# Chunk 2 of a fused layernorm + MLP + long convolution enters the MLP already transposed, with row statistics from ScalarE

## The chip, the cores and the metric

One core of one Trainium2 chip. The metric is the time of one execution in microseconds (us); the number given for a kernel is the median over its runs.

## What is computed

All numbers are float32. S = 2048 rows, D = 448 columns, F = 1792 hidden columns.

```python
x  = A_q
xn = layernorm(x)                       # per row: (x - mean) / sqrt(var + 1e-5)
# part A: gated long convolution
k_shift = sum_t pad(k)[t:t+S] * shift_k[:, 3-t]        # causal, 4 taps, per column
kv = k_shift * v
y  = causal_conv(kv, ssm_k) + kv * ssm_D               # length S, per column, by FFT
A  = xn * y
# part B: MLP
h  = xn @ w1 + b1
B  = mish(h) @ w2                       # mish(h) = h * tanh(softplus(h))
out = x + A + B
```

## The kernel before, in words

**The MLP sets the frame.** The 2048 rows are eight chunks of 256 rows, and the 14 blocks of 128 hidden columns are seven pairs, so there are 56 (chunk, pair) steps, each of two *slots*: slot 2i issues step i's first layer (`g1_mm`, line 544, 22 matmuls), slot 2i+1 its activation (`mish`, line 547) and the second layer of step i-2 (`g2_mm`, lines 576 to 578, 12 matmuls). Each product is made from high and low float32r parts, so every operand is split: a copy to the high part on ScalarE, a subtraction for the low part on VectorE (`split`, lines 89 and 90). Chunk c begins at slot 14c; chunk 2 at slot 28.

**The convolution is woven in between.** In slots 6 to 59, eight groups of k and v and eight groups of the filter go through a first transform: `f1_mm` (line 154) multiplies a group into two two-bank accumulators named pq and pr; `f1_fold` then empties them, ScalarE copying one (line 160) and VectorE adding and subtracting the other (line 164, two instructions); `f1_out` stores the result. There is one pair pq, pr for all groups, so the next `f1_mm` waits for the fold before it. VectorE also makes kv from k and v (`taps`, lines 192 to 211); GpSimd multiplies one tap of each group (line 190). In the stretch that matters here the order of the multiplies is: filter group 5 (slot 20), kv group 0 (24), filter group 6 (26), kv group 1 (29). The second stage and the inverse follow from slot 59 on.

**How a chunk gets its normalised, transposed input.** The first layer needs xn with columns on partitions. There are two ways, and `NT` says where the second begins.

- Chunks below NT (0, 1 and 2 before): the chunk is loaded with rows on partitions (`ln_load`). `ln_stats` (line 451) puts the row statistics on VectorE (line 430 twice, 433 twice, 436) into a queue that is emptied between other VectorE instructions; the last entry of the queue gives GpSimd a power, two normalisations and two small copies (lines 439, 443, 447). `ln_T` (line 510) has TensorE transpose the tile in two halves of four instructions each (`transposes`, line 496), and ScalarE and VectorE split it from the accumulator (lines 508, 506).
- Chunks from NT on (3 to 7 before): the rows are still loaded, as the residual and for the statistics, but the transposed chunk comes from a second copy of the input, `qT` (`xT_load`, line 458, into the single tile XN). `nt_stats` (line 460) has ScalarE make two passes over each of the two row blocks, a sum and a sum of squared differences (lines 466 to 468, four large and some small instructions); GpSimd makes the reciprocal root (469, 470) and stores mean and root of all 256 rows, 2 KB, to DRAM (474). `nt_row` (477) loads the 128 pairs of one half back, broadcast to all partitions, into the one tile `idr`. `nt_norm` (483) subtracts and multiplies on VectorE, and `nt_split` (490, 491) makes the two parts. There is a second row load for the second half; it fills the same tile, so it waits until the first half's `nt_norm` has read it.

**What sets the order.** The order on every engine is written out by hand: `at(slot, ...)` calls are issued at the start of a slot and `after(slot, ...)` calls at its end, each engine takes its instructions in that order, and SyncE's queue of loads and stores is one such order. Where the k, v and filter groups are loaded is in lines 628 to 652. The steps of a chunk c from NT on are placed here, from the tables of the diff:

```python
    for c in range(NT, NCHUNK):
        at_ = NT_HOW.get(c, NT_AT)
        b = 2 * NP * (c - 1) + (1 if c < 5 else 0)
        at(b + at_["q"], ln_load, c)
        at(b + at_["x"], xT_load, c)
        after(NT_STATS[c], nt_stats, c)
        for jj in range(2):
            at(b + at_["row"][jj], nt_row, c, jj)
            after(b + at_["norm"][jj], nt_norm, c, jj)
            after(b + at_["split"][jj], nt_split, c, jj)
```

Of the kernel before, what the change touches and what calls it, by code (L numbers as in the profile page):

```python
# [29 lines left out]
I2_AT = {100: ((6, 7, 0, 1), 92, (95, 97, 98, 99), (0, 2, 0, 1)),  # L30
         108: ((2, 3, 4, 5), 101, (104, 105, 106, 107), (0, 1, 0, 1))}
LATE = 2
NT = 3
NT_AT = {"q": -5, "x": -1, "stats": -2, "flush": 0, "row": (4, 8), "norm": (7, 10), "split": (8, 11)}
NT_SOON = dict(NT_AT, row=(4, 5), norm=(4, 7), split=(6, 8))
NT_HOW = {c: dict(NT_SOON) for c in (4, 7)}
NT_HOW[6] = dict(NT_AT, row=(4, 10), norm=(8, 11), split=(9, 13))
NT_HOW[7]["x"] = 0
NT_HOW[3] = dict(NT_SOON, q=-9, stats=-3, flush=-2)
NT_HOW[5] = dict(NT_AT, q=-8, stats=-4, flush=-2)  # L40
NT_STATS = {3: 27, 4: 41, 5: 53, 6: 70, 7: 82}
EVAC_SOON = 2,
WARM_N = (448, 448, 448)
FILL_N = (224, 112, 96)
# [3 lines left out]
def tile_kernel(ctx: ExitStack, tc, q, qT, k, v, sk, hT, sD, w10, w1, w2, c_fib, c_g, c_gi, c_i2, out):  # L48
# [20 lines left out]
    E = dp.tile([NJ * 4, 64, D], F32, name="E")  # L69
    MR = {c: dp.tile([2, CH], F32, name="MR") for c in range(NT, NCHUNK)}  # L70

# [8 lines left out]
    def rs(c):  # L80
        return rstd[:, 2 * c:2 * c + 2] if c < NT else mv[:, 2 * c:2 * c + 2, 1]

# [37 lines left out]
    def at(slot, fn, *args):  # L120
        plan.setdefault(int(slot), []).append((fn, args))

    def after(slot, fn, *args):
        plan2.setdefault(int(slot), []).append((fn, args))
# [294 lines left out]
    def xn_tile():  # L419
        return mp.tile([128, 4, CH], F32, name="xn", bufs=1)  # L420

    def ln_parts(c):
        st = mp.tile([128, 2, 6], F32, name="bst", bufs=2)
        ve = mp.tile([128, 2], F32, name="ve", bufs=2)
        if c < NT:
            XN[c] = xn = xn_tile().rearrange("p a b -> p (a b)").rearrange("p (j d) -> p j d", j=2)
# [83 lines left out]
    def ln_T(c, jj):  # L510
        if jj == 0:
            dv(len(drip))
            x_tiles(c)
        p = pg()
        transposes(c, jj, p)
        for lo in range(2):
            x_split(c, jj, p, lo)
# [73 lines left out]
    def mlp_slot(s):  # L591
# [3 lines left out]
        if half == 0:  # L595
            if i < n:
                c, p = pairs[i]
                if c + 1 < NT:
                    if p == 0:
# [8 lines left out]
        else:  # L608
            if i < n:
                c, p = pairs[i]  # L610
                if p == NP - 2 and c + 1 < NT:
                    ln_T(c + 1, 0)
# [83 lines left out]
# [8 lines that stand above are left out]
# [152 lines left out]
```

## Time and profile before

| What | Value |
|---|---|
| median of 3 runs (lowest to highest) | 357.65 us (357.64 to 357.86) |
| the profiled execution | 357.91 us, span of its instructions 356.1 us |
| VectorE (DVE) busy | 282.0 us, 79% |
| ScalarE (ACT) busy | 160.1 us, 45% |
| GpSimd (POOL) busy | 72.4 us, 20% |
| DMA | 83.27 MB, mean 234 GB/s |
| granted TensorE clock, mean | 1.000 |

How to read it: PE is TensorE, DVE VectorE, ACT ScalarE, POOL GpSimd; SPq, ACTq and POOLq are the queues in which SyncE, ScalarE and GpSimd issue transfers. A row of the timeline has the start in us from the span's first instruction, the duration in us, engine, source line, operation, output<-inputs with their shapes, a count, and in brackets how long the engine was idle before it and what ended the idle time. Neighbouring instructions of an engine overlap a little at their ends, so that the distance from one start to the next is what an instruction costs its engine.

### The profile page before, as it was taken

The page shows a single profiled execution, that of the slowest core. Times are in us where ns is not written, and L with a number is a line of the kernel's source. Part 1 is how long each engine was busy: PE and PEld are TensorE (multiplying, and loading weights), DVE is VectorE, ACT ScalarE, POOL GpSimd, SP SyncE. Part 2 cuts the span into 40 slices and gives each one's busy share as a digit, 9 for nine tenths or more (in the row PEclk, how much of TensorE's full clock was granted, in tenths as well). Part 3 has the DMA queues.
Part 4 walks back from the last instruction along what each step waited for, and adds up shares of the span by engine and source line. Part 5 has one row for each costly group of instructions (what it writes and reads, how often), then busy time and mean ns, then how long its engine had stood idle before and what let it go on. Part 6 is the DMA issues. An engine that isn't in the chain of part 4 may idle for free.

```text
span 356.1 us, 7495 instructions
## 1 busy us (share of the span) xinstructions
PE 350.7 (98%) x3092; PEld 289.1 (81%) x3092; DVE 282.0 (79%) x374; ACT 160.1 (45%) x308; POOL 72.4 (20%) x83
## 2 busy tenths in 40 slices
PE   8999999999999999999999999999999999999995
PEld 2988888888888989888987568657756799979794
DVE  5989748998999999997539868868985963788941
ACT  3975652347343643373232732333634333354470
POOL 2037002822310250222000120110310016040030
PEclk9999999999999999999999999999999999999999
DMA  7999976949769356664859488879756467989086
GB/s 247 344 374 305 401 307 164 352 113 249 209 178 314 127 153 175 218 162 107 246 180 356 135 309 285 254 229 380 257 151 240 105 175 263 407 335 272 17 119 139
DMA packets 30691, 83.27 MB, mean 234 GB/s; under 512 B 3137, under 2 KB 15810, under 8 KB 30658
## 3 DMA queue, kind: packets, MB, share of 16 engines
q1 hardware_dynamic: 21842, 47.82, 39.6%
q0 software_dynamic: 4928, 22.95, 20.3%
q10 hardware_dynamic: 3888, 12.03, 13.1%
q8 instruction: 24, 0.39, 0.4%
q14 instruction: 9, 0.07, 0.1%
HBM read 54.34 MB, written 28.45 MB: 232 GB/s over the span
## 4 chain that ended last, share of the span: by engine, by line
PE 96%; DMA 2%; ACT 1%; SPq 0%; issue 0%; DVE 0%
PE pg L544 23%; PE pg L576 13%; PE pg L578 13%; PE pg L577 13%; PE pa L544 6%; PE pq L544 5%; PE pq L154 4%; PE pa L298 3%; PE pr L544 3%; PE pq L243 3%; PE pr L243 3%; PE pp L544 2%; DMA kr<-in_w_dram 2%; PE pa L243 1%; PE pp L352 1%; PE pb L544 1%
## 5 line engine op out<-in xcount | busy, mean ns | idle before, releaser
L576 PE MATMUL pg<-w2h,ach 128*128 128x448 f32 x224 | 82.2, 367 | 0.0
L578 PE MATMUL pg<-w2h,acl 128*128 128x448 f32 x224 | 81.3, 363 | 0.0
L577 PE MATMUL pg<-w2l,ach 128*128 128x448 f32 x224 | 81.2, 362 | 0.0
L90 DVE TENSOR_TENSOR acl<-a,ach 128x512 fp32r<-128x512 f32 x56 | 38.9, 694 | 34.3 <-ACT ach L89 34.2
L544 PE MATMUL pg<-XH,w1h 128*128 128x256 f32 x264 | 52.9, 284 | 0.1
L552 ACT ACTIVATE a<-pg,b1t 128x256 f32<-128x256 f32 x66 | 27.9, 472 | 55.0 <-PE pg L544 42.9
L576 PEld LDWEIGHTS pg<-w2h,ach 128*128 128x128 f32 x224 | 42.0, 187 | 9.5 <-issue 5.0
L544 PEld LDWEIGHTS pg<-XH,w1h 128*128 128x128 f32 x264 | 41.5, 188 | 7.2 <-issue 5.6
L578 PEld LDWEIGHTS pg<-w2h,acl 128*128 128x128 f32 x224 | 42.0, 188 | 2.5
L577 PEld LDWEIGHTS pg<-w2l,ach 128*128 128x128 f32 x224 | 42.1, 188 | 2.3
L544 PE MATMUL pg<-XL,w1h 128*128 128x256 f32 x264 | 42.9, 277 | 0.0
L164 DVE TENSOR_TENSOR st<-pq,st 128x896 f32<-128x896 f32 x32 | 34.8, 1089 | 4.7 <-ACT st L160 3.9
L544 PEld LDWEIGHTS pg<-XL,w1h 128*128 128x128 f32 x264 | 35.9, 188 | 0.0
L89 ACT CAST ach<-a 128x512 fp32r<-128x512 f32 x56 | 34.8, 621 | 1.7
L544 PE MATMUL pg<-XH,w1l 128*128 128x256 f32 x198 | 33.6, 278 | 0.0
L190 POOL TENSOR_TENSOR x<-kr,skb 128x896 f32<-128x896 f32 x8 | 17.0, 2130 | 71.0 <-PE pr L154 26.2
L309 POOL DMA_DIRECT2D E<-qe x14 | 8.8, 632 | 94.2 <-ACT qe L252 94.2
L207 DVE TENSOR_TENSOR x<-x 128x896 f32<-128x896 f32 x24 | 26.2, 1091 | 2.0 <-POOL x L190 1.4
L544 PEld LDWEIGHTS pg<-XH,w1l 128*128 128x128 f32 x198 | 27.6, 188 | 0.0
L160 ACT COPY st<-pr 128x896 f32<-128x896 f32 x16 | 14.5, 907 | 13.5 <-PE pr L154 11.5
L552 ACT ACTIVATE a<-pa,b1t 128x256 f32<-128x256 f32 x16 | 6.7, 472 | 30.3 <-PE pa L544 30.3
L154 PE MATMUL pq<-x,con 32*64 32x448 f32 x128 | 15.9, 560 | 0.0
(171 smaller groups left out, 639.2 us busy)
## 6 DMA issues: line engine op xcount, KB each, us to landing
Dkv<-st ACTq DMA_DIRECT2D x16, 448.0 KB, 5.2
ah<-Dh SPq DMA_DIRECT2D x8, 896.0 KB, 8.3
av<-Dkv SPq DMA_DIRECT2D x8, 896.0 KB, 8.7
e<-E POOLq DMA_DIRECT2D x8, 896.0 KB, 7.4
E<-qe POOLq DMA_DIRECT2D x14, 448.0 KB, 6.9
kr<-in_k_dram SPq DMA_DIRECT2D x10, 448.0 KB, 6.1
Dh<-st ACTq DMA_DIRECT2D x10, 448.0 KB, 6.8
x<-in_hT_dram SPq DMA_DIRECT2D x8, 448.0 KB, 6.4
```

Of the source, the lines that this page charges most:

```text
L89: nc.scalar.copy(h, raw)
L90: V.tensor_sub(l, raw, h)
L154: nc.tensor.matmul(ps[h][64 * jj:64 * jj + 64, b, :D], f1[rg:rg + 32], x[rg:rg + 32, jj], start=True, stop=True, tile_position=(rg, 64 * jj))
L164: f(st[:, n], e, st[:, 1])
L190: nc.gpsimd.tensor_mul(o, KR[g - u // 2], skb[:, u:u + 1].to_broadcast([128, 2, D]))
L207: V.tensor_add(KV[g], KV[g], o)
L243: nc.tensor.matmul(bk(p, r)[32 * t:32 * t + 32, :D], g[rs, t, c], a[rs, t], start=True, stop=True, tile_position=(64 * r, 32 * t))
L544: nc.tensor.matmul(ps[n], l, r, start=all(m[0] != n for m in seq[:n_]), stop=all(m[0] != n for m in seq[n_ + 1:]))
L552: nc.scalar.activation(a[:, n], ps[n], AF.Mish, bias=b1t[:, 2 * p + n:2 * p + n + 1])
L576: nc.tensor.matmul(ps, ah[:, n, cs], w2h[:, f], start=f == 0, stop=False)
L577: nc.tensor.matmul(ps, ah[:, n, cs], w2l[:, f], start=False, stop=False)
L578: nc.tensor.matmul(ps, al[:, n, cs], w2h[:, f], start=False, stop=f == NF - 1)
```

## The change

`NT` falls from 3 to 2: chunk 2 takes the second way. Its own placing is added. With b = 15 for chunk 2, the rows are loaded at slot 14 (as before), the transposed chunk at slot 16, the statistics are issued after slot 15, the broadcast rows at slots 18 and 21, the normalisations after slots 20 and 22, the splits after slots 22 and 24.

```diff
-NT = 3
+NT = 2
 NT_AT = {"q": -5, "x": -1, "stats": -2, "flush": 0, "row": (4, 8), "norm": (7, 10), "split": (8, 11)}
 NT_SOON = dict(NT_AT, row=(4, 5), norm=(4, 7), split=(6, 8))
 NT_HOW = {c: dict(NT_SOON) for c in (4, 7)}
+NT_HOW[2] = dict(NT_AT, q=-1, x=1, row=(3, 6), norm=(5, 7), split=(7, 9))
 NT_HOW[6] = dict(NT_AT, row=(4, 10), norm=(8, 11), split=(9, 13))
...
-NT_STATS = {3: 27, 4: 41, 5: 53, 6: 70, 7: 82}
+NT_STATS = {2: 15, 3: 27, 4: 41, 5: 53, 6: 70, 7: 82}
```

What goes with it: chunk 2's eight transposes, its statistics on VectorE and its normalisation on GpSimd. What comes: a 512 KB load of `qT`, the two passes on ScalarE, the 2 KB store, two broadcast loads of 128 KB on SyncE's queue, and four VectorE instructions (line 483).

## The prediction

> **What bounds the kernel.** I read the span and clock first, then on the page the engines and the chain that ended last.
>
> ```profile
> core 0: 356.1 us, clock 1.000
> ```
>
> ```profile
> PE 350.7 (98%) x3092; PEld 289.1 (81%) x3092; DVE 282.0 (79%) x374; ACT 160.1 (45%) x308; POOL 72.4 (20%) x83
> PE 96%; DMA 2%; ACT 1%; SPq 0%; issue 0%; DVE 0%
> ```
>
> TensorE is busy 98% of the span and 96% of the chain: from the first steps to the end it waits for nothing. So an edit pays what it takes off TensorE, and costs every pause that it puts there. The profiled execution took 357.91 us, 0.26 above the median of 357.65; I reckon differences in its trace and add them to the median.
>
> **What is removed from TensorE.** TensorE's timeline around the two halves of chunk 2's transposes:
>
> ```profile
> 73.86 0.60 PE L496 MATMUL pg<-con,xn 128*128 128x128 f32 x4
> 74.22 0.45 PE L576 MATMUL pg<-w2h,ach 128*128 128x448 f32 x1
> ...
> 76.81 0.59 PE L154 MATMUL pq<-x,con 32*64 32x448 f32 x2
> ...
> 77.74 0.66 PE L496 MATMUL pg<-con,xn 128*128 128x128 f32 x4
> 78.16 0.60 PE L544 MATMUL pg<-XH,w1h 128*128 128x256 f32 x3
> ```
>
> Start to start, the first half costs 74.22 - 73.86 = 0.36 us and the second 78.16 - 77.74 = 0.42. The saving is 0.8 us, 0.22% of the time; 0.2% (0.72 us) is about what a measurement of this kernel can tell from no change. It stands only if nothing new makes TensorE wait. The row between the halves, 76.81, is the multiply of filter group 6. It writes pq and pr, so it needs the fold of kv group 0 to be over, and this is VectorE's deadline. Without the first half of the transposes TensorE would be there at 76.81 - 0.36 = 76.45.
>
> **How late VectorE can be.** Its timeline from the fold of filter group 5 on:
>
> ```profile
> 57.92 0.62 DVE L430 BATCH_NORM_STATS2 bst<-qt 128x6 f32<-128x448 f32 x1
> ...
> 61.38 1.09 DVE L164 TENSOR_TENSOR st<-pq,st 128x896 f32<-128x896 f32 x1 [1.09 <-ACT st L160]
> ...
> 62.51 1.09 DVE L164 TENSOR_TENSOR st<-pq,st 128x896 f32<-128x896 f32 x1
> 63.51 1.11 DVE L207 TENSOR_TENSOR x<-x 128x896 f32<-128x896 f32 x1
> 64.61 1.05 DVE L90 TENSOR_TENSOR acl<-a,ach 128x512 fp32r<-128x512 f32 x1
> 65.59 0.61 DVE L200 TENSOR_TENSOR x<-kr,skb 128x448 f32<-128x448 f32 x1
> 66.12 0.61 DVE L202 TENSOR_TENSOR x<-kr,skb 128x448 f32<-128x448 f32 x1
> 66.77 1.09 DVE L207 TENSOR_TENSOR x<-x 128x896 f32<-128x896 f32 x1
> 67.89 1.50 DVE L210 TENSOR_TENSOR x<-x 128x896 f32<-128x896 f32 x1
> 69.31 1.08 DVE L197 TENSOR_TENSOR x<-kr,skb 128x896 f32<-128x896 f32 x1
> ...
> 74.27 1.09 DVE L164 TENSOR_TENSOR st<-pq,st 128x896 f32<-128x896 f32 x1
> ```
>
> The last row is the second half of the fold of kv group 0; it ends at 75.36. From 61.38 on no idle time stands in these rows: VectorE works without a break towards a deadline that, at 76.45, is 1.1 us away. The row at 69.31 is the first instruction of kv group 1 and the first to read that group's k.
>
> **What the change adds there.** The same steps of chunk 3 show the price:
>
> ```profile
> 103.82 1.41 DVE L483 TENSOR_TENSOR xn<-xn,con 128x512 f32<-128x512 f32 x2
> 105.16 1.08 DVE L164 TENSOR_TENSOR st<-pq,st 128x896 f32<-128x896 f32 x1
> ...
> 112.44 0.68 DVE L491 TENSOR_TENSOR XL<-xn,XH 128x512 fp32r<-128x512 f32 x1
> 113.04 1.41 DVE L483 TENSOR_TENSOR xn<-xn,con 128x512 f32<-128x512 f32 x2
> ```
>
> One half's normalisation takes 105.16 - 103.82 = 1.34 us of VectorE and one low part 113.04 - 112.44 = 0.60. By the slots, the first normalisation (after 20) goes in behind the add at 63.51; the first low part and the second normalisation (both after 22) behind the instruction at 69.31. So 1.34 + 0.60 + 1.34 = 3.28 us come in ahead of the deadline. The low parts replace two that were made from the accumulator later and are no new work, but the first is now earlier than the deadline. Some time is given back, because GpSimd no longer normalises beside VectorE:
>
> ```profile
> 63.51 2.77 POOL L443 TENSOR_SCALAR xn<-qt,mv,rstd 128x448 f32<-128x448 f32 x1
> ```
>
> Beside it the subtraction at 64.61 took 65.59 - 64.61 = 0.98, where 0.60 is usual for its shape (112.44), and the multiply at 67.89 took 1.42, where 62.51 to 63.51 shows 1.00. That is 0.8 us. The statistics that leave VectorE (57.92 and its like) lie ahead of the wait at 61.38, which ScalarE's copy ends, so that they buy nothing later.
>
> **ScalarE's two passes** come in front of the copy that empties filter group 4:
>
> ```profile
> 47.46 0.94 ACT L89 CAST w2h<-x 128x896 fp32r<-128x896 f32 x1
> 49.47 0.91 ACT L160 COPY st<-pr 128x896 f32<-128x896 f32 x1 [1.07 <-PE pr L154]
> ...
> 83.29 0.58 ACT L466 ACTIVATE a<-qt 128x448 f32<-128x448 f32 x1 [0.75 <-DVE st L164]
> ...
> 86.53 0.19 ACT L468 ACTIVATION_READ_ACCUMULATOR a<-qt,mv 128x1 f32 x1
> ```
>
> For chunk 3 they take from 83.29 to 86.72, 3.4 us. Issued behind the cast of 47.46 they run from 48.4 to 51.8, and the copy of 49.47 and VectorE's fold behind it are 2.3 us late. VectorE meanwhile has two statistics less (2 x 0.6) and the 1.09 us of waiting at 61.38: together 2.3, so this delay is covered at about nothing; without that cover it would add up to 1 us to what follows.
>
> **The row's way and who stands behind it.** First SyncE's queue; then GpSimd's store of chunk 3, and five answers on the time from issue to landing, in this order: of the stores, of the row loads up to 141 us, of the one k load issued at 105.64, of all k loads, and of the loads of qT.
>
> ```profile
> 56.43 0.35 SPq L589 DMA_DIRECT2D out_dram<-qt  x1
> 60.66 0.33 SPq L414 DMA_DIRECT2D qt<-in_q_dram  x1
> 61.51 0.42 SPq L180 DMA_DIRECT2D kr<-in_k_dram  x1
> ...
> 94.72 0.33 SPq L477 DMA_DIRECT2D con<-MR  x1
> ...
> 105.26 0.32 SPq L477 DMA_DIRECT2D con<-MR  x1
> 105.64 0.83 SPq L180 DMA_DIRECT2D kr<-in_k_dram  x1
> ```
>
> ```profile
> 88.81 0.85 POOL L474 DMA_DIRECT2D MR<-mv  x1 [0.30 <-POOL mv L470]
> DMA to landing us min/median/max: 3.7/6.0/7.3
> DMA to landing us min/median/max: 3.0/4.8/5.5
> DMA to landing us min/median/max: 5.6/5.6/5.6
> DMA to landing us min/median/max: 3.5/6.1/13.2
> DMA to landing us min/median/max: 4.1/9.4/10.0
> ```
>
> For chunk 3 the store follows the end of the passes by 88.81 - 86.72 = 2.1 us; here it goes out at 53.9, lands at 59.9 (57.6 to 61.2), and only then can SyncE issue the first row, which lands 4.8 later, at 64.7 (60.6 to 66.7). VectorE is ready for it at 64.5. So the first normalisation runs from 64.7 to 66.0. All that while SyncE's queue stands still, with slot 18's row at its head. Chunk 0's output (56.43) goes out at 60.1, and the load of chunk 3's rows (60.66), which needs that tile, about 64.3. Then comes the second row load (slot 21): it fills the tile that the normalisation reads, so it waits until 66.0, exactly as 105.26 waits for the end of 103.82's pair. Behind it in the queue stands the k load of kv group 1 (slot 22): 61.51 before, 66.4 now. With the 5.6 us of the load that went out behind a row at 105.64 it lands at 72.0; with the bounds 3.5 and 6.1 (the median of all) at 69.9 to 72.5. I take 5.6, being the same position in the queue.
>
> VectorE gets to kv group 1 at 66.0 + (69.31 - 64.61) - 0.8 = 69.9. It waits 2.1 us, until 72.0 instead of 69.31: 2.7 late. With the low part and the second normalisation the fold is 2.7 + 0.60 + 1.34 = 4.6 late and ends at 80.0. TensorE, ready at 76.45, pauses 3.5 us.
>
> **The sum.** Multiply of filter group 6 at 80.0 instead of 76.81: +3.2 (the first half of the transposes is swallowed in it). Second half: -0.4. Total +2.8: 360.7 for an execution like the profiled one, 360.4 on the median. What follows is late by the same amount and not by more: in this order VectorE waits at the end of kv group 1 for ScalarE again, so that its lag ends there. The load of qT (slot 16) stands in the queue ahead of the row's wait; issued at any time before 54 it is there at 64.7 even with the longest landing of its kind, 10.0 us, and costs nothing; issued later it would join the row's lateness.
>
> A rule of the Trainium skill bears on a pause of that length. "TensorE: Matmul & The Clock Gate", section "The HAM clock gate (the 'warmup' mystery)", says that after an idle window of about 3.4 us the clock falls to half until TensorE has been busy for as long. By that rule the sum would be about 1.7 us more, +4.5. The granted clock here is 1.000 in the mean, and no row of before shows a pause of this kind, so the rule is untried in this case; my sum goes without it.
>
> **The rivals.**
>
> - *The k load is in time* (lands by 69.9). Then only VectorE's added work counts: 3.28 - 0.8 = 2.5 late, or 2.7 with the row at 64.7, the fold ends at 77.8 to 78.0, and the total is +0.6 to +0.8 with the saving, or +0.5 with an earlier row: 358.2 to 358.4, about no change to slightly slower. For it: the fastest k load took 3.5 us. Against: chunk 3's rows of q, a filter group and this k now start within 2 us of each other. 0.21, of it 0.13 within 0.2%.
> - *The fold is in time* (ends by 76.45), and the whole 0.8 us stays: 356.8, faster. VectorE would need 1.4 us beyond the 1.1 of slack and the 0.8 given back, and the k load in time as well. It could come from GpSimd's leaving: all of VectorE's instructions from 62 to 71 us ran beside it, and I have credited two. It decides at 76.45. 0.17, of it 0.15 faster.
> - *Store and row are slow* (7.3 and 5.5): the first normalisation ends at 68.0, the k load at 6.1 lands at 74.5, the total is +5.3: 363.0. 0.07.
> - *The clock drops* for about as long as the pause, 3.5 us at half pace: another 1.8 us, 362.2. For it: a pause of this length is nowhere in the trace, so that nothing shows the clock holding through one. Against: it is 1.000 in the mean. The length at which it decides isn't to be had from these rows. 0.05. (The page of the Trainium skill named above puts it at about 3.4 us.)
>
> **How the numbers follow.** My forecast has 0.50, its own range 359.0 to 361.2. Faster is the second rival's 0.15; within 0.2% is 0.13 + 0.02; slower is 0.08 + 0.50 + 0.07 + 0.05 = 0.70. The range from 356.7 to 361.8 holds the forecast and the first two rivals and leaves out the last two, with the forecast's tail.
>
> **What would show it.** Right: no transpose (line 496) for chunk 2; a pause of TensorE of about 3.5 us ahead of line 154 near 76 us, released by VectorE's line 164; ahead of that VectorE idle for about 2 us at line 197, released by the k load; SyncE issuing the row of line 477 near 60 and near 66, the k load directly behind the second. Wrong: line 154 starts near 76.4 with no pause (the second rival), or the pause is there without the wait on the k load (the first), or VectorE waits for the row itself at line 483 by more than a microsecond (the third).

## The result, and the profile after

The changed kernel takes 364.36 us (median of 5 runs, 362.72 to 365.03) against 357.65: slower by 1.8%, ratio 1.0176, interval 1.0164 to 1.0189. The profiled execution took 364.8 us. Executions of this kernel, and of several below, differ among themselves by whether the granted TensorE clock falls after a pause; each such number therefore stands with the clock of its execution. Of these five, 362.72 and 363.35 us ran at a mean clock of 0.995 and 364.36 to 365.03 at 0.991.

Span and clock first; then from the page the engines, the chain that ended last and the granted clock in 40 slices.

```profile
core 0: 362.7 us, clock 0.991
```

```profile
PE 352.6 (97%) x3084; PEld 290.0 (80%) x3084; DVE 282.5 (78%) x373; ACT 163.2 (45%) x318; POOL 65.7 (18%) x81
...
PEclk9999999987999999999999999999999999999999
...
PE 91%; DMA 3%; DVE 3%; issue 1%; SPq 0%; ACT 0%
```

TensorE has eight instructions fewer, the transposes, and yet is busy 1.9 us longer; a DMA and VectorE have come into the chain; and the clock dips in two slices, between 72 and 91 us. TensorE's timeline at the multiply of filter group 6 (at 76.81 before), and VectorE's from the fold of filter group 5 to the end of that of kv group 0:

```profile
81.20 1.01 PE L155 MATMUL pq<-x,con 32*64 32x448 f32 x2 [4.71 <-DVE st L165]
```

```profile
61.46 2.22 DVE L165 TENSOR_TENSOR st<-pq,st 128x896 f32<-128x896 f32 x2 [1.41 <-ACT st L161]
63.59 1.08 DVE L208 TENSOR_TENSOR x<-x 128x896 f32<-128x896 f32 x1
64.59 1.41 DVE L484 TENSOR_TENSOR xn<-xn,con 128x512 f32<-128x512 f32 x2
...
68.83 1.09 DVE L211 TENSOR_TENSOR x<-x 128x896 f32<-128x896 f32 x1
73.19 1.09 DVE L198 TENSOR_TENSOR x<-kr,skb 128x896 f32<-128x896 f32 x1 [3.27 <-DMA kr<-in_k_dram]
74.20 0.68 DVE L492 TENSOR_TENSOR XL<-xn,XH 128x512 fp32r<-128x512 f32 x1
74.81 1.41 DVE L484 TENSOR_TENSOR xn<-xn,con 128x512 f32<-128x512 f32 x2
...
80.06 1.09 DVE L165 TENSOR_TENSOR st<-pq,st 128x896 f32<-128x896 f32 x1
```

VectorE enters kv group 1 late (line 198, 69.31 before) because k isn't there: 3.27 us without work. The normalisation of 74.81 and the low part of 74.20 follow, so the fold ends at 81.15 instead of 75.36 and TensorE pauses 4.71 us. Where k was: SyncE's queue, and behind it GpSimd's store and ScalarE's passes.

```profile
56.74 0.33 SPq L478 DMA_DIRECT2D con<-MR  x1
57.28 0.41 SPq L590 DMA_DIRECT2D out_dram<-qt  x1
63.41 0.33 SPq L415 DMA_DIRECT2D qt<-in_q_dram  x1
...
66.03 0.33 SPq L478 DMA_DIRECT2D con<-MR  x1
66.41 0.43 SPq L181 DMA_DIRECT2D kr<-in_k_dram  x1
```

```profile
52.94 0.81 POOL L475 DMA_DIRECT2D MR<-mv  x1 [0.29 <-POOL mv L471]
```

```profile
48.13 0.57 ACT L467 ACTIVATE a<-qt 128x448 f32<-128x448 f32 x1
...
51.46 0.88 ACT L161 COPY st<-pr 128x896 f32<-128x896 f32 x1
```

The second row load waits for the normalisation that begins at 64.59, and the k load goes out right behind it at 66.41, 4.9 us later than before. Last, the stretch from 76 us on (columns: window, its length, busy time of PE, PEld, DVE, ACT and POOL, PEclk, DMA share, GB/s):

```profile
76.00:78.00 2.00, 0.49 (x3) 0.12 (x1) 1.97 (x5) 1.72 (x4) 0.00 (x0) 1.00 0.32 129
78.00:80.00 2.00, 0.00 (x0) 0.00 (x0) 2.00 (x3) 0.26 (x1) 0.85 (x1) 0.95 0.00 0
80.00:82.00 2.00, 0.80 (x8) 0.33 (x16) 1.85 (x3) 0.00 (x0) 1.23 (x1) 0.50 0.00 0
82.00:84.00 2.00, 2.00 (x21) 1.07 (x6) 2.00 (x4) 0.89 (x1) 0.00 (x0) 0.50 0.33 38
84.00:86.00 2.00, 2.00 (x11) 2.00 (x11) 1.93 (x4) 0.01 (x1) 0.00 (x0) 0.50 0.94 372
86.00:88.00 2.00, 2.00 (x14) 1.96 (x13) 1.97 (x3) 0.54 (x2) 0.00 (x0) 0.85 0.85 309
```

The eighth column is the clock: half from 79.8 (a tenth of the second window) to 86.6, 6.8 us in all, although TensorE works again from 81.2.

**Where the 6.9 us lie.** Comparing the starts of the same matmuls in the two traces: 0.17 early up to 56 us, 0.07 late from 57, 0.38 early at 75 (the first transposes saved), 4.39 late at the multiply of filter group 6, 6.42 late behind the half clock, and 6.41 to 6.49 from there to the end. So all of the loss but the 0.24 us at 57 arises between 76 and 88 us. The pause makes 4.39; the half clock makes 6.42 - 4.39 + 0.42 (the second transposes, saved there too) = 2.45. The span is 6.6 longer, and the remaining 0.3 lies outside it.

### The profile page after: what moved, and what is told of

It reads as the page before. It is cut to its first block, busy times and chain, and to the rows that moved or that the text cites. A ratio compares the mean times of both kernels' runs of the same rounds, so it can differ in the third digit from the quotient of the medians.

```text
span 362.7 us, 7491 instructions
## 1 busy us (share of the span) xinstructions
PE 352.6 (97%) x3084; PEld 290.0 (80%) x3084; DVE 282.5 (78%) x373; ACT 163.2 (45%) x318; POOL 65.7 (18%) x81
## 4 chain that ended last, share of the span: by engine, by line
PE 91%; DMA 3%; DVE 3%; issue 1%; SPq 0%; ACT 0%
PE pg L545 22%; PE pg L577 12%; PE pg L579 12%; PE pg L578 12%; PE pa L545 6%; PE pq L545 5%; PE pq L155 4%; PE pa L299 3%; PE pr L545 3%; PE pr L244 3%; PE pq L244 3%; PE pp L545 2%; DMA kr<-in_k_dram 2%; DMA x<-in_hT_dram 2%; PE pa L244 1%; DVE st L165 1%
## 5 line engine op out<-in xcount | busy, mean ns | idle before, releaser
L578 PE MATMUL pg<-w2l,ach 128*128 128x448 f32 x224 | 81.2, 362 | 0.0
L155 PE MATMUL pq<-x,con 32*64 32x448 f32 x128 | 16.7, 586 | 4.8 <-DVE st L165 4.7
```

The lines of the kernel that those rows point to most:

```text
L155: nc.tensor.matmul(ps[h][64 * jj:64 * jj + 64, b, :D], f1[rg:rg + 32], x[rg:rg + 32, jj], start=True, stop=True, tile_position=(rg, 64 * jj))
L578: nc.tensor.matmul(ps, ah[:, n, cs], w2l[:, f], start=False, stop=False)
```

## Experiments

The theory after this comparison: the time is lost in two steps. The fold of kv group 0 is late, because VectorE has 3.3 us more to do ahead of it with 1.1 to spare, and because the k load is held in SyncE's queue; and the pause then halves the clock. The rivals: that one of the two causes does it alone, that ScalarE's passes delay the chain from the start, and that the clock had nothing to do with it. Each experiment names the times of before that shared its chip. Three of the sixteen expectations met the time that they gave (filler4, hold_alone, row2_behind_k); the other thirteen kernels came out slower than expected. A trace is of one execution, and already at 20 us its matmuls start up to 0.6 us earlier or later than those of before.

### The clock by itself

**filler4**: the changed kernel with four idle products in the pause.

```diff
     def f1_mm(src, g, key):
         x = src.pop(g)
+        if (key, g) == ("h", 6):
+            warmer = pg()
+            for _ in range(4):
+                nc.tensor.matmul(warmer[0:8, 0:448], wz, wz[:, 0:1].to_broadcast([128, 448]), start=True, stop=True)
```

> The changed kernel with four idle multiplies (448 columns of zeros, about 0.75 us each, result unused) ahead of the multiply of filter group 6, in the pause. Theory (the pause halves the clock for some microseconds after it, and this costs about 2.4 us beside the pause itself): the pause ends where it did, the granted clock stays 1.0, time 361.5 to 362.3. Rival (the lower clock costs nothing by itself, the pause and VectorE's lag are the whole loss): time within 0.5 us of 364.4.

Measured: 361.68 us (361.05 to 362.08), before 357.74, ratio 1.0105 (1.009 to 1.012). TensorE stands idle for only 0.4 us and keeps its clock, 0.998 or more in all four executions. The profile is of the fastest; TensorE's wait and VectorE's timeline:

```profile
PE pq L159 <- DVE st L169: 0.4, 1, 0.4
```

```profile
72.05 1.09 DVE L202 TENSOR_TENSOR x<-kr,skb 128x896 f32<-128x896 f32 x1 [2.07 <-DMA kr<-in_k_dram]
...
78.92 1.09 DVE L169 TENSOR_TENSOR st<-pq,st 128x896 f32<-128x896 f32 x1
```

By the medians the half clock cost 364.36 - 361.68 = 2.7 us and the late fold the other 3.9. In this execution k landed sooner than in the profiled one of the changed kernel: VectorE waits 2.07 us for it instead of 3.27, and the fold ends at 80.01 instead of 81.15. The two profiled executions differ by 364.8 - 361.05 = 3.75 us; less these 1.14, the half clock is 2.6, near the 2.45 of the trace. This execution, with k in use 5.6 us after its issue and the clock full, is also the prediction's own sum put to the test: the fold was forecast to end at 80.0.

### One part of the change on the kernel before

**vector_alone**: VectorE's added work and nothing else; the products are not used.

```diff
+    def extra(n):
...
+        o, i = XS[2][1][:, :, 0:128], skb[:, :, 0:128]
+        m = skb[:, 1, 0:256].rearrange("p (a t) -> p t a", t=2)[:, 0:1].to_broadcast([128, 4, 128])
+        for _ in range(n):
+            V.tensor_tensor(o, i, m, op=ALU.mult)
...
+    after(20, extra, 2)
+    after(22, extra, 3)
```

> The kernel before with five VectorE multiplies of 128x512 added, two after slot 20 and three after slot 22 (at some 0.65 us each about 3.2 us, the added VectorE work of the change), written into a tile that chunk 2 doesn't use yet; the results are unused and everything else, the transposes too, stays as before. My theory: VectorE's deadline at the multiply of filter group 6 had about 1.1 us to spare, so this work alone makes a pause of about 2 us at that multiply, 359.4 to 359.9, with the k load on time (issued near 61.5) and, the pause being under 2.5 us, the full clock; one half-clock window would make it 360.6 to 361.2. Rival, that VectorE's work is hidden and only the late k load costs: no pause at line 154, under 358.2.

Measured: 360.1 us (359.78 to 361.97), before 357.77, ratio 1.0077 (1.0051 to 1.0103). Three executions at a clock of 0.999 or more took 359.8 to 360.2; the profiled one, at 0.995, took 361.97. TensorE's pause, a short wait behind it and the windows of that one:

```profile
78.92 0.59 PE L154 MATMUL pq<-x,con 32*64 32x448 f32 x2 [1.45 <-DVE st L164]
```

```profile
PE pg L553 <- DVE XL L514: 0.2, 1, 0.2
```

```profile
80.00:82.00 2.00, 1.77 (x10) 1.53 (x11) 2.00 (x5) 1.39 (x2) 0.00 (x0) 0.71 0.44 65
82.00:84.00 2.00, 2.00 (x11) 2.00 (x11) 1.93 (x3) 0.00 (x0) 0.00 (x0) 0.50 0.98 363
```

VectorE's work alone makes the multiply 2.1 us late (0.2 of it stands in this trace from 20 us on), and costs 2.0 to 2.4 at the full clock, with the k load on time. The five products take 3.7 us of VectorE here, a little more than the 3.28 that they stand for. The forecast that a pause under 2.5 us leaves the clock alone failed here: a pause of 1.45 us and, 1.6 us behind it, a wait of 0.23 for chunk 2's low part were followed by half clock for 3.4 us.

**hold_alone**: SyncE's queue held and nothing else, by a small store that has to wait for kv group 0.

```diff
...
+    at(21, lambda: nc.sync.dma_start(Hd, KV[0][0:1, 0]))
```

> The kernel before with one small store added to SyncE's queue at slot 21, of one row of kv group 0's tile to a scratch row, which has to wait for VectorE's last write of that tile near 64.6: the queue stands still until then, and the k load of kv group 1 goes out about 3.4 us later, near 64.9, with no work added to any engine. My theory: the hold of the queue makes the k load late by itself. It then lands at 70 to 72.5, VectorE waits 0.7 to 3.2 us for it, TensorE pauses up to 2 us at line 154: 358.0 to 359.7. Rival, that a held queue costs nothing here because a k load that doesn't share DMA with a store lands in under 5 us: it lands by 69.5, no pause, 357.7 to 358.1.

Measured: 358.31 us (357.94 to 359.56), before 357.77, ratio 1.0023 (1.0013 to 1.0033). The profile is of the fastest execution. There the k load goes out at 64.63 and lands 5.4 us later; VectorE's timeline:

```profile
67.48 1.09 DVE L208 TENSOR_TENSOR x<-x 128x896 f32<-128x896 f32 x1 [1.06 <-DMA Hd<-x]
...
70.08 1.09 DVE L198 TENSOR_TENSOR x<-kr,skb 128x896 f32<-128x896 f32 x1 [0.38 <-DMA kr<-in_k_dram]
```

It loses 1.06 us to the added store (a wait that the change doesn't have) and 0.38 to k, and TensorE waits for nothing: that is what VectorE has to spare. So a hold of 3.1 us by itself is nearly hidden, and the 0.5 us of the median is at the low end of what was expected. The two causes share one slack, and neither gives the pause of the changed kernel in these two runs. The changed kernel holds k for 4.9 us; a hold of that length alone was not made, and k that lands as late as there gives most of the pause by itself (rows_gpsimd_no_norm).

**passes_alone** and **passes_behind**: ScalarE's two passes over chunk 2's rows and nothing else, their sums not used; after slot 15, ahead of the copy of filter group 4, or after slot 16, behind it.

```diff
...
+    after(15, passes, 2)
```

```diff
...
+    after(16, passes, 2)
```

> The kernel before with one part of the change alone: ScalarE's two passes over chunk 2's rows after slot 15, their results unused. Theory (VectorE's wait for ScalarE's next copy absorbs the later fold of filter group 4): nothing, 357.5 to 357.9. Rival (the passes delay the chain of folds): 358.3 or more.

Measured: 359.01 us (357.91 to 359.7), before 357.85, ratio 1.0027 (1.0013 to 1.0041). The expectation of no cost failed. SyncE's queue and VectorE in the profiled execution:

```profile
57.49 0.35 SPq L598 DMA_DIRECT2D out_dram<-qt  x1
62.44 0.33 SPq L414 DMA_DIRECT2D qt<-in_q_dram  x1
...
64.58 0.42 SPq L180 DMA_DIRECT2D kr<-in_k_dram  x1
```

```profile
71.70 1.09 DVE L197 TENSOR_TENSOR x<-kr,skb 128x896 f32<-128x896 f32 x1 [1.76 <-DMA kr<-in_k_dram]
```

The fold of filter group 4 is late, chunk 0's output goes out 1.1 us later and takes longer to land, the load of q that needs its tile goes out at 62.44 instead of 60.66, and k at 64.58 instead of 61.51, beside the store of filter group 5. The kernel before still has the statistics on VectorE, so the cover that the change brings is missing here.

> The kernel before with ScalarE's two passes alone, results unused, but one slot later, so that they stand behind the copy that empties filter group 4 instead of ahead of it. Theory (ahead of the copy they delayed fold, store of the filter group and chunk 0's output, and with that output the loads behind it, which cost 1.2 us in the run with the passes alone): the copy goes at its old time, chunk 0's output near 56.5 and the k load of kv group 1 near 61.5 to 62; 357.5 to 358.1, no change. Rival (the passes cost ScalarE time that the kernel lacks wherever they stand): 358.6 or more.

Measured: 358.55 us (358.37 to 359.07), before 357.88, ratio 1.0022 (1.0013 to 1.0031). k goes out at 62.77, lands at 68.7 and nobody waits for it; TensorE loses 0.41 us at 57 us, where VectorE empties chunk 0's accumulator late. So passes cost 0.7 to 1.2 us where nothing is taken off VectorE ahead of them. By the starts of the matmuls, 0.24 of it is lost at 57 us in passes_alone; in passes_behind 0.69 is, which is the whole cost.

### One part of the change undone or moved

**rows_gpsimd**: chunk 2's row loads from GpSimd's queue, so that they hold nothing of SyncE's.

```diff
-        nc.sync.dma_start(idr, MR[c][jj].partition_broadcast(128))
+        (nc.gpsimd if c == 2 else nc.sync).dma_start(idr, MR[c][jj].partition_broadcast(128))
```

> The changed kernel, but chunk 2's two broadcast rows are loaded from GpSimd's queue instead of SyncE's. Theory (the k load of kv group 1 is late because it stands behind the rows in SyncE's queue): the k load goes out near 62.5 instead of 66.4, VectorE no longer waits 3.3 us for it, only the added VectorE work delays the fold; TensorE pauses about 1.5 us instead of 4.7, the clock stays full, time 358.0 to 358.7. Rival (the transfer engines are the limit, whatever the queue): the k load still lands after 71.5, VectorE still waits over 1.5 us, time 359.5 or more.

Measured: 361.26 us, before 357.74, ratio 1.012 (1.008 to 1.0159); by execution 359.56 at a clock of 1.0, 360.97 at 0.999, 361.56 at 0.995, 363.91 at 0.991. In the profile, the one at 1.0, SyncE, VectorE and TensorE's wait:

```profile
64.51 0.42 SPq L181 DMA_DIRECT2D kr<-in_k_dram  x1
```

```profile
69.81 1.08 DVE L198 TENSOR_TENSOR x<-kr,skb 128x896 f32<-128x896 f32 x1
...
72.36 1.42 DVE L484 TENSOR_TENSOR xn<-xn,con 128x512 f32<-128x512 f32 x2 [0.87 <-DMA con<-MR]
```

```profile
PE pq L155 <- DVE st L165: 2.3, 1, 2.3
```

k lands 4.5 us after its issue and is in time (69.81 without a wait), so the pause is halved. What is left is VectorE's work, and 0.87 us for the second row, which GpSimd issues late. Against filler4, both without the half clock, the hold of SyncE's queue was worth 361.68 - 359.56 = 2.1 us by this execution, 0.7 by the one at 0.999, and 361.05 - 359.56 = 1.5 between the two profiled ones.

**row2_behind_k**: only the second row load is moved, behind the k load of kv group 1.

```diff
-NT_HOW[2] = dict(NT_AT, q=-1, x=1, row=(3, 6), norm=(5, 7), split=(7, 9))
+NT_HOW[2] = dict(NT_AT, q=-1, x=1, row=(3, 7), norm=(5, 7), split=(7, 9))
```

> The changed kernel, but chunk 2's second row is loaded one slot later, so that in SyncE's queue it stands behind the k load of kv group 1 instead of ahead of it. Theory of the queue: the k load goes out near 65 instead of 66.4 (chunk 0's output and chunk 3's rows still hold it) and lands near 71; the pause of TensorE falls by about 2 us to under 3 us, the clock stays full, time 359.0 to 360.0. Rival (the second row in the queue doesn't matter, the transfers before it do): k load lands near 73 as before, time above 363.

Measured: 359.53 us (358.7 to 363.3, 10 runs), before 357.74, ratio 1.0071 (1.0042 to 1.0101). k goes out at 65.05 and lands at 70.2 without a wait; the second row costs 0.82 us; the pause is 2.48. Executions at a clock of 0.998 or more took 358.7 to 359.8, those at 0.995 or less 361.6 to 363.3. The profiled one is of the second kind; its windows:

```profile
76.00:78.00 2.00, 0.68 (x4) 0.29 (x2) 1.98 (x3) 0.23 (x1) 0.89 (x1) 1.00 0.41 167
78.00:80.00 2.00, 0.84 (x16) 0.24 (x16) 1.87 (x2) 0.00 (x0) 1.19 (x1) 0.93 0.00 0
80.00:82.00 2.00, 2.00 (x15) 1.58 (x8) 2.00 (x5) 0.91 (x1) 0.00 (x0) 0.50 0.34 45
82.00:84.00 2.00, 2.00 (x15) 2.00 (x14) 1.93 (x4) 0.00 (x0) 0.00 (x0) 0.71 0.98 355
```

The half clock lasts 0.28 + 2 + 1.16 = 3.4 us, one window. One changed number in the placing takes 4.8 us off the median of the changed kernel: 2.2 of it is the shorter pause (2.48 instead of 4.71), the rest less half clock, which all five executions of the changed kernel show and four of these ten.

**passes16**: the changed kernel with the passes after slot 16, behind the copy of filter group 4.

```diff
-NT_STATS = {2: 15, 3: 27, 4: 41, 5: 53, 6: 70, 7: 82}
+NT_STATS = {2: 16, 3: 27, 4: 41, 5: 53, 6: 70, 7: 82}
```

> The changed kernel with the passes one slot later, behind the copy of filter group 4. Theory (two separate things make the k load late, the passes ahead of the copy and the rows in SyncE's queue): the copy is on time, but the store of mean and root lands 2.3 us later, near 59, and SyncE's queue stands until then, so that chunk 0's output still goes out near 59 and the k load after 66; the pause stays about 4 us or more, 362.5 to 365. Rival (the passes' place is the whole cause): k load before 63, time under 360.

Measured: 370.35 us (369.74 to 370.94), before 357.88, ratio 1.035 (1.0336 to 1.0363). The first row goes out only when the store has landed, and the rest of SyncE's queue behind it:

```profile
62.99 0.33 SPq L478 DMA_DIRECT2D con<-MR  x1
63.41 0.38 SPq L590 DMA_DIRECT2D out_dram<-qt  x1
...
70.37 1.71 SPq L181 DMA_DIRECT2D kr<-in_k_dram  x1
```

```profile
PE pq L155 <- DVE st L165: 7.6, 1, 7.6
```

k goes out 4 us later than in the changed kernel, the pause is 7.6 us, and the clock is half for three windows in all executions (0.986). This is the hold of the queue at its plainest, but not the later passes alone: the store is issued 3.1 us later than in the changed kernel, and it took 6.9 us to land instead of 3.8.

**late_norm**: the second normalisation and both splits moved behind the fold of kv group 0, the rows left in SyncE's queue.

```diff
+NT_HOW[2] = dict(NT_AT, q=-1, x=1, row=(3, 6), norm=(5, 9), split=(9, 10))
```

> The changed kernel, but the second normalisation and the low part of the first half come after the fold of kv group 0 instead of before it (slots 24 and 25); the rows stay in SyncE's queue. Theory (the pause is the wait for the k load plus 3.28 us of added VectorE work ahead of the fold): 1.94 us less stand ahead of the fold, the pause falls from 4.7 to about 2.8 us, the clock stays full, time 359.3 to 360.2. Rival (VectorE's added work is hidden in its wait for the k load): pause and time as in the changed kernel, 363 to 365.

Measured: 362.98 us (361.81 to 364.04), before 357.74, ratio 1.0142 (1.0118 to 1.0167). 1.94 us of VectorE's work have left, but k lands at 73.9 (7.3 us after its issue), VectorE waits 3.79 for it and the pause is still 3.3. The one execution at a clock of 1.0 took 361.81.

**rows_gpsimd_no_norm**: rows from GpSimd's queue, and chunk 2's four normalising instructions left out, so that chunk 2 enters the MLP unnormalised.

```diff
     def nt_norm(c, jj):
+        if c == 2:
+            return
```

> Rows of chunk 2 from GpSimd's queue, and chunk 2's subtraction and multiplication (four VectorE instructions) left out, so that chunk 2 enters the first layer unnormalised. Theory: the fold of kv group 0 ends near 75, no pause, 356.7 to 357.1: everything else that the change brought (load of qT, ScalarE's passes, store, rows) costs nothing. Rival (one of those costs as well): 357.6 or more.

Measured: 362.14 us (359.6 to 363.81), before 357.85, ratio 1.0112 (1.008 to 1.0144): the expectation failed. VectorE in the profile:

```profile
73.42 1.09 DVE L198 TENSOR_TENSOR x<-kr,skb 128x896 f32<-128x896 f32 x1 [4.68 <-DMA kr<-in_k_dram]
```

k went out at 64.43, early enough, but between the two halves of the store of filter group 5 (64.08 and 64.73) and behind a row (63.34), and took 9.0 us. So the experiment shows something else than it was made for: a late k with no normalisation behind it, the first low part alone, gives a pause of 3.6 us.

**gpsimd_norm**: the normalisations on GpSimd, the rows in its queue, the splits late.

```diff
...
-            V.tensor_tensor(x, x, m, op=op)
-            dv()
+            (nc.gpsimd if c == 2 else V).tensor_tensor(x, x, m, op=op)
+            if c > 2:
+                dv()
```

> Rows of chunk 2 from GpSimd's queue, chunk 2's four normalising instructions on GpSimd instead of VectorE, both low parts behind the fold of kv group 0. Theory (TensorE pauses only because VectorE gets work that it has no slack for): VectorE keeps the slack that it had before, no pause near 76 or 85, the whole 0.8 us of the transposes stays: 356.7 to 357.2, faster than before. Rival (GpSimd beside VectorE slows it by more than its slack, or GpSimd is too slow for the split): a pause again, 357.6 or more.

Measured: 360.96 us (360.3 to 364.7), before 357.85, ratio 1.0108 (1.0075 to 1.0141). VectorE has nothing to normalise, and its other work runs longer beside GpSimd:

```profile
65.27 1.79 DVE L91 TENSOR_TENSOR acl<-a,ach 128x512 fp32r<-128x512 f32 x1
...
74.17 2.09 DVE L208 TENSOR_TENSOR x<-x 128x896 f32<-128x896 f32 x1
```

These took 0.69 and 1.09 in the changed kernel. VectorE also waits 0.98 us for k, which took 6.9 us. The pause is 1.79 us; part of the work came back as slower work.

### Other placings

**rows_gpsimd_late**: rows from GpSimd's queue and late_norm's placing together.

> Both edits together: rows of chunk 2 from GpSimd's queue, and the second normalisation and the first low part behind the fold of kv group 0. Theory (with the k load in time, what is left is VectorE's work ahead of its deadlines): 1.94 us and the 0.9 us wait for the second row leave the stretch ahead of the fold, which then ends near 75.9, ahead of TensorE's 76.45, so that the pause there is gone; the work moves in front of the fold of filter group 6, which can make a second pause of about 0.5 us near 85; clock full, time 357.2 to 357.9. Rival (the moved work delays the next deadline by all of its 1.94 us): 358.4 to 359.

Measured: 359.87 us (359.43 to 362.22), before 357.85, ratio 1.0068 (1.0045 to 1.0092). The pause at the fold is gone; TensorE now waits for chunk 2's low part itself:

```profile
85.01 0.38 PE L545 MATMUL pg<-XL,w1h 128*128 128x256 f32 x1 [0.79 <-DVE XL L492]
```

**early** and **early_sync**: q loaded at slot 11, the passes after 13, the normalisations after 19 and 22, the splits after 24 and 25; the rows from GpSimd's queue or from SyncE's.

```diff
+NT_HOW[2] = dict(NT_AT, q=-4, x=1, row=(2, 5), norm=(4, 7), split=(9, 10))
...
+NT_STATS = {2: 13, 3: 27, 4: 41, 5: 53, 6: 70, 7: 82}
```

> The changed kernel with the same work placed earlier: chunk 2's rows loaded at slot 11 instead of 14, the passes after slot 13 instead of 15, the broadcast rows from GpSimd's queue at slots 17 and 20, the first normalisation after slot 19, where VectorE waited for ScalarE, the second after 22, both low parts behind the fold of kv group 0. Theory (k load on time, and only 1.34 us of added VectorE work ahead of the deadline at the multiply of filter group 6, of which GpSimd's leaving gives back 0.8): no pause near 76, clock full, the 0.8 us of the transposes stay: 356.7 to 357.3, faster than before. Rival (VectorE has no room for the normalisation anywhere in this stretch): pause of over 0.8 us, 357.7 or more.

Measured: 359.93 us (359.68 to 361.41), before 357.88, ratio 1.0068 (1.0055 to 1.0082); not the gain that was expected. The 2 KB store landed 8.2 us after its issue, so that VectorE waited 1.96 for the first row; the pause is 1.1 us, and TensorE waits 0.4 for kv group 0 ahead of it and 0.7 for chunk 1's evacuation behind it.

> The same early placing, but with the rows in SyncE's queue as in the change. Theory (rows hurt there only while they hold later loads back): the first row waits for the store until about 53 and holds nothing that is due, the second waits for the normalisation until about 61.5, which is when the k load went out before; k load near 62, the pause under 0.5 us, 356.8 to 357.6. Rival (any row in SyncE's queue makes the k load late enough for a pause): 358 or more.

Measured: 360.86 us (359.89 to 362.44), before 357.88, ratio 1.0089 (1.0066 to 1.0112): 359.9 to 360.0 at the full clock. k goes out at 64.17, VectorE waits 1.46 for it, the pause is 2.7.

**early2**: as early, the second normalisation after slot 24, behind the fold of kv group 0.

```diff
+NT_HOW[2] = dict(NT_AT, q=-4, x=1, row=(2, 6), norm=(5, 9), split=(8, 9))
```

> The changed kernel with chunk 2's rows of q loaded at slot 11, the passes after slot 13, the row loads in GpSimd's queue at slots 17 and 21, the normalisations after slots 20 and 24 and the splits after slots 23 and 24: only the first normalisation and the first split lie ahead of the fold of kv group 0, the second normalisation after the fold. My theory, that the loss is the sum of a late k load and of VectorE's work ahead of that deadline: both are mostly gone, the k load goes out near 61.7, VectorE has 1.9 us more instead of 3.3 against 1.1 to spare, the pause is under 1 us and the clock full, 357.2 to 358.4. Rival, that the new way of chunk 2 costs as much wherever it is put, since VectorE has no slack up to the chunk's start either: over 358.8, with waits of TensorE for the fold or for the parts of chunk 2 that add up to more than 1.5 us.

Measured: 359.56 us (359.36 to 360.85), before 357.77, ratio 1.0061 (1.0039 to 1.0082). The multiply of filter group 6 starts without a pause at 76.06, with the saving in hand. The next deadline, the multiply of kv group 1, isn't met; TensorE and ScalarE there:

```profile
86.86 0.59 PE L155 MATMUL pq<-x,con 32*64 32x448 f32 x2 [2.17 <-DVE st L165]
```

```profile
78.62 0.62 ACT L491 CAST XH<-xn 128x512 fp32r<-128x512 f32 x1 [6.69 <-DVE xn L484]
```

ScalarE's cast of the second half stands at the head of its order and waits 6.69 us for the normalisation; the activation behind it is late, and VectorE waits 0.69 and 0.70 us for ScalarE.

**early3**: as early2, the second half's split issued after slot 25's activation, ahead of that slot's taps.

```diff
+    after(25, nt_split, 2, 1)
...
+            if (c, jj) != (2, 1):
+                after(b + at_["split"][jj], nt_split, c, jj)
```

> The kernel of the placing before this one (rows of q at slot 11, passes after 13, row loads in GpSimd's queue, second normalisation after slot 24) with one change: the second half's split is issued after slot 25's activation instead of ahead of it, and ahead of slot 25's taps on VectorE. There ScalarE's cast for the high part stood in front of that activation and waited 6.7 us for the normalisation, so that VectorE waited 0.69 and 0.70 us for ScalarE and the fold of filter group 6 ended 2.2 us late. My theory: both waits of VectorE go, the fold ends about 85.2, the pause ahead of the multiply of kv group 1 is about 0.6 us instead of 2.17, and the time is 357.2 to 358.3, within 0.2% of the kernel before. Rival: VectorE's 3.3 us more work up to that multiply is the bound whatever the order, the pause stays at 1.5 us or more and the time over 358.6.

Measured: 358.63 us (358.13 to 359.29, 11 runs), before 357.89, ratio 1.0019 (1.001 to 1.0028).

```profile
85.61 0.59 PE L155 MATMUL pq<-x,con 32*64 32x448 f32 x2 [0.79 <-DVE st L165]
```

Both waits are gone and the pause falls from 2.17 to 0.79 us, as the order of ScalarE's queue explains it. The time is a little above the expected one. This is the best placing found, 5.7 us better than the change as made, and it doesn't beat the kernel before: up to the multiply of kv group 1, VectorE's added work just about eats the 0.8 us.

## Why the prediction was wrong

The sign and the mechanism held: a pause ahead of line 154, released by the fold, behind a wait of VectorE for k, behind SyncE's held queue. The amount was 4 us short, outside the range. By its own steps:

- **The saving**, 0.8 us: right. TensorE is 0.45 us earlier at 75 us than at 68, as early2 shows without a pause 0.8 us earlier at 81.
- **VectorE's deadline and its work**: right to 0.1 us. VectorE came to kv group 1 at 69.92 (forecast 69.9), and from the landing of k to the end of the fold it took 81.15 - 73.19 = 7.96, where 6.05 + 1.94 was forecast. By vector_alone this work, without the 0.8 that GpSimd's leaving returns, makes the multiply 2.1 us late.
- **ScalarE's passes "covered at about nothing"**: they ran from 48.13 to 51.46 as forecast, and VectorE's fold of filter group 5 began at 61.46 instead of 61.38, so the cover held at that fold. The 0.24 us at 57 us got past it. Without the cover (passes_alone, passes_behind) 0.7 to 1.2 us, where up to 1 was forecast.
- **The store and the rows**: the store took 3.8 us and not 6.0, and the first row could go out at 56.74. It was of no use: the normalisation had to wait for VectorE until 64.59 (forecast 64.7), the second row for the normalisation (66.03, forecast 66.0), and k went out at 66.41 (forecast 66.4). That these times met the forecast although the store's landing did not is luck: VectorE's lag, and not the row's landing, set them.
- **"With the 5.6 us of the load that went out behind a row at 105.64 it lands at 72.0" failed.** k took 6.7 us, above the upper bound of 6.1 that was its median. The load at 105.64 had the same place in the queue, but not the same company: here chunk 3's rows, a filter group and both halves of the store of filter group 5 went out within 3 us of it, and from 70 to 76 us the DMA share is 1.01. But filler4 has the same company (store at 66.09, k at 66.46), and there k was in use 5.6 us after its issue (72.05). So the step that failed is to take one landing, with a median for its upper bound, for a load that took 4.5 (rows_gpsimd) to 9.0 us over these runs; what made it 6.7 here is not shown. The late 1.15 us went whole into the pause: 4.71 instead of 3.5, the multiply 4.39 late instead of 3.2.
- **"My sum goes without it": the clock.** It had a chance of 0.05 and cost 2.45 us by the trace, 2.6 to 2.7 by filler4. A mean clock of 1.000 in a trace without pauses is no evidence of what a pause does, and it was counted as such. The rule of the Trainium skill ("TensorE: Matmul & The Clock Gate", section "The HAM clock gate (the 'warmup' mystery)") named the right effect; the measurement differs from it in the size of the idle time, in the last section.
- **"Late by the same amount and not by more"**: right, 6.41 to 6.49 from 88 us to the end.

Together: 2.8 forecast, 1.15 from the landing, 2.45 from the clock, 0.2 in the rest of the span and 0.3 outside it, which is the 6.9 of the profiled execution. Where neither step failed, in the profiled execution of filler4, the fold ends at 80.01 (forecast 80.0) and the matmuls stay 2.87 us late (forecast 2.8). The rival with k in time had the right mechanism and too low a price: 358.2 to 358.4 forecast, 359.56 measured in rows_gpsimd at the full clock, where the second row came 0.87 us too late. The rival with the fold in time was put at 356.8 and held only as far as that deadline: rows_gpsimd_late, early2 and early3 meet it and lose the saving at the next one; they take 0.7 to 2.0 us more than the kernel before.

Open remains why k's landing varies as it does. Issued 1.2 us or more ahead of the store of filter group 5 it took 4.5 us (rows_gpsimd), 5.2 (row2_behind_k) and 5.9 to 6.3 in six others; less than 1 us ahead of it 7.1 to 7.3 (passes_alone, early_sync, rows_gpsimd_late); between or behind the store's halves 5.4 (hold_alone) to 9.0. The longest landings are all beside or behind the store, but its company gives no fixed amount, and no run isolated it.

## What to carry to other kernels

An edit that saves 0.8 us of the bound engine has to be priced at each deadline of the engine that takes over its work, and along every in-order queue it is put in: here a small row load that waits for a landing and then for a normalisation held back a large load that had nothing to do with it. Price a transfer's landing by what goes out beside it, with the longest landing of its kind as the bound and not the median, and give a pause of the bound engine beyond a microsecond or two its price in clock. When a placing is hand-written, look first for the instruction that stands at the head of a queue with nothing to do: moving one row load was worth 4.8 us with the half clock that it avoided, one cast 0.9.

## What the hardware showed that was not expected

- **The half clock comes in whole windows of 3.4 us and for less than such a window of idle time.** It lasted 6.8 us in the changed kernel, 3.4 in row2_behind_k and vector_alone, 10.2 in passes16. The windows keep their own time: from the fall of the clock in the pause to its fall behind the last matmul it is 279.89 us in row2_behind_k, late_norm, early_sync and rows_gpsimd_no_norm, and 283.31 in the changed kernel, 82 and 83 times 3.4133, whatever stood between. Going back one window from the first fall, TensorE had been idle for 3.3 us of it in the changed kernel (and for 1.4 of the next, which was again followed by half clock), 2.48 in row2_behind_k, 1.68 in vector_alone (1.45 and 0.23).
- **The idle time of a window doesn't decide by itself.** The section of the Trainium skill named above speaks of an idle window of about 3.4 us and of windows that run free of the program; the second agrees with these runs, the first is too long for them. The clock stayed full after 2.31 us in rows_gpsimd; counted back from the fall of the clock at the end of that trace, a boundary at 77.7 divides this pause into 1.2 and 1.1. It also stayed full with 1.6 us idle in one window of early2, and with 1.9 in the window of rows_gpsimd_late that holds its last matmuls, more than the 1.68 above, so that something else than idle time counts too. In vector_alone the rest of the window is nearly all the multiply by 32-row tiles and transposes; that these count for little activity is a guess that no run tested. The clock of rows_gpsimd differs from execution to execution, from 1.0 at 359.56 us to 0.991 at 363.91; that the pause lies differently in the windows is the likely reason, but only one execution of each kernel has a trace.
- **Four idle products are enough to keep the clock**, worth 2.6 to 2.7 us here, and they are no help to a kernel that should not pause at all.
- **The landing of one and the same 448 KB load** went from 4.5 to 9.0 us, and of the 2 KB store from 3.8 to 8.2, over these runs. What goes out beside them differs from run to run, but does not settle it: k took 6.7 us in the changed kernel and at most 5.6 in filler4, in the same company.
- **VectorE's 128x512 subtraction took 1.79 us instead of 0.69** beside a normalisation on GpSimd, and its 128x896 addition 2.09 instead of 1.09.
